# Summing seven tap products in PSUM on TensorE instead of on VectorE, for the first two blocks of a convolution with two MLPs

## The chip, the cores and the metric

One core of one Trainium2 chip. The metric is the time of one execution on the device in microseconds; the median of some runs is compared. The engines that matter here are PE (matmul; its weight loads, PEld, overlap it), VectorE (DVE in the rows), ScalarE (ACT) and the queue SP, which issues nearly all DMAs. PE reads its operands from SBUF and writes PSUM; VectorE and ScalarE read and write both.

## The reference

x is [2, 4096, 192], weight_gen is [2, 4096, 8, 7]; all is float32. Over the seven taps of each token and head a softmax is taken, and each token's output is the weighted sum of the seven tokens that end with it (zeros ahead of the sequence), 8 heads of 24 channels. Then two MLPs follow, 192 to 2048 to 192, with different activations.

```python
w = exp(weight_gen - max(weight_gen, axis=-1))
w = w / (sum(w, axis=-1) + 1e-9)
out[b, s, h, :] = sum over k of w[b, s, h, k] * x_pad[b, s + k, h, :]
x = out.reshape(8192, 192)
h = x @ moe_w_in;   x = maximum(0.01 * h, h) @ moe_w_out
h = x @ moe2_w_in;  x = maximum(h, 0) ** 2 @ moe2_w_out
```

## The kernel before

The 8192 tokens are 16 blocks of 512 (tb). A block is held as 128 partitions by 4 tokens (TB) by 192 channels for the sum over taps, and as channels by 512 tokens for the MLPs. For these every float32 operand is split into a high part (rounded to fp32r) and a low part (the rest): `xah`, `xal` hold channels 0 to 127 of a block, and `xbh`, `xbl` hold channels 128 to 191 twice, in partitions 0 to 63 and again in 64 to 127, so that two matmuls of 64 rows can run side by side as a pair. `halves` makes such a split: ScalarE casts (L359), VectorE subtracts (L366).

A block of one layer has 8 steps of 256 hidden units. A step forms `ph` (two PSUM banks) from x and the first weights (L518), ScalarE makes `gh` and `g` of it (L636 and L637 in layer one), VectorE subtracts `gl` (L644), and two steps later (LAG) PE adds the second product into `pa` and `pb` (L534). The list `steps` begins with three steps of block 0 (AHEAD = 3), then steps of blocks 1 and 0 alternate. So steps 0 to 2 belong to block 0, step 3 is the first of block 1. Steps 0 and 1 form only `ph` (nine units of matmuls); from step 2 on a step is 19 pairs.

`local_sum` makes the sum over taps of a block on VectorE: the softmax (L407 to L422), seven products, each of `xc` (the block with its halo) and one tap of `wg`, broadcast over 24 channels (L430), and an addition of each product after the first to `att` (L438). Products go through `tmp`, a ring "c" of two buffers. Then the sum has to be turned from tokens by channels to channels by tokens. Blocks 0 and 1 (`tb < EARLY`) have it turned by PE: ScalarE copies channels 128 to 191 once more behind the others (L443), and eight transposes of 128 by 128 (L451) write two tiles `pt`, for the a part and the b part. `pt` shares the PSUM ring "ph" of two slots with `ph`. The later 14 blocks are turned by VectorE's 32 by 32 transpose (L461) and a round trip through DRAM.

At the start the weights of both layers are also loaded and split (`piece`): ScalarE L283, VectorE L288 and L294, ScalarE L300, VectorE L304, then ScalarE L318 and VectorE L328 write the high and low parts. Each piece is one or two of the eight parts of a matrix.

The order of instructions on each engine is fixed when the program is built, by the class `Plan`. Every operation gives an engine, a cost in us, a priority, and the buffers that it reads and writes. PE takes its operations strictly in order of priority. The other engines take, by the planned times, the operation with the smallest priority unless another can start more than 0.15 us earlier. A buffer of a ring is given when its last user has ended in the plan. On the chip an engine works through its list in order and waits for semaphores. The products and additions have priority `pr - 2`, the transposes `at[0, tb] - 0.45` (just ahead of the block's first step), `gl` of step s has s + 1.2. For block 2 the products and additions have priority 10, ahead of the `gl` of step 9, which has 10.2. A second `xc` or `wg` is loaded when the products of the block before have been done, since each has one buffer.

Of the kernel before, what the change touches and what calls it, by code (L numbers as in the profile page):

```python
# [8 lines left out]
F32 = mybir.dt.float32  # L9
# [5 lines left out]
ALU = mybir.AluOpType  # L15
# [125 lines left out]
def kernel(  # L141
# [17 lines left out]
    nc = tc.nc  # L159
# [3 lines left out]
    B, S, D = x.shape  # L163
    H, K = weight_gen.shape[2], weight_gen.shape[3]
    G = D // H
    FF = w_in1.shape[1]
    NT = B * S
    P = 128
    HALO = K - 1
    TB = 4  # L170
    N = TB * P
    NTB = NT // N
    A = 32
# [4 lines left out]
    Q = 64  # L178
# [16 lines left out]
    def act(n):  # L195
        return 0.17 + n / 1200

    def dve(n):
        return (n + 151) / 960
# [166 lines left out]
            lambda: nc.vector.tensor_tensor(lo.t, v(), h.t.bitcast(F32), op=ALU.subtract),  # L366
        )

    AW = 4 * Q

    def local_sum(tb, pr, gate=()):
        xc = pl.buf(sb, [P, HALO + TB, D], F32, "xc", "xc", 1)
        wg = pl.buf(sb, [P, TB, H, K], F32, "wg", "wg", 1)
        mx = pl.buf(sb, [P, R, 1], F32, "mx", "mx", 1)
        sm = pl.buf(sb, [P, R, 1], F32, "sm", "sm", 1)
        att = pl.buf(sb, [P, TB, AW], F32, "att", "att", 1)
        xs = sets[0, tb] = x_set()

        xv = lambda: xc.t.rearrange("p t d -> p (t d)")

        def load_w():
            for i in range(BI):
                (nc.sync if tb else nc.scalar).dma_start(
                    out=wg.t[i * A : (i + 1) * A].rearrange("p t h k -> p (t h k)"), in_=wg_flat[i, :, tb]
                )

        def load():
            q = nc.sync
            if tb == 0:
                nc.gpsimd.memset(xc.t[0 : 2 * A, 0:HALO, :], 0.0)  # L390
            for i in range(BI):
                z = max(HALO - TB * i, 0) if tb == 0 else 0
                q.dma_start(out=xv()[i * A : (i + 1) * A, z * D :], in_=window(i, 0, A, tb, z, HALO + TB))
                for b in range(B if z else 0):
                    a0 = b * APB + 1
                    q.dma_start(  # L396
                        out=xv()[i * A + a0 : i * A + a0 + APB - 1, : z * D], in_=window(i, a0, APB - 1, 0, 0, z)
                    )

        pl.op("SP" if tb else "ACT", 2.0, pr - 10, [], [wg], load_w, after=gate, late=(0.4, 2.0))  # L400
        pl.op("SP", 2.0 if tb else 4.0, pr - 10, [], [xc], load, after=gate, late=(3.6, 2.0))

        def w2():
            return wg.t.rearrange("p t h k -> p (t h) k")

        n = R * K
        pl.op("DVE", dve(n), pr - 3, [wg], [mx], lambda: nc.vector.tensor_reduce(mx.t, w2(), axis=AX.X, op=ALU.max))  # L407
        pl.op(
            "DVE", dve(n), pr - 3, [wg, mx], [wg],
            lambda: nc.vector.tensor_tensor(w2(), w2(), mx.t.to_broadcast([P, R, K]), op=ALU.subtract),  # L410
        )
        pl.op("ACT", act(n), pr - 3, [wg], [wg], lambda: nc.scalar.activation(w2(), w2(), AF.Exp))

        def norm():
            nc.vector.tensor_reduce(sm.t, w2(), axis=AX.X, op=ALU.add)
            nc.vector.tensor_scalar_add(sm.t, sm.t, 1e-9)
            nc.vector.reciprocal(sm.t, sm.t)

        pl.op("DVE", dve(n) + 0.45, pr - 3, [wg], [sm], norm)
        pl.op(  # L420
            "DVE", dve(n), pr - 3, [wg, sm], [wg],
            lambda: nc.vector.tensor_tensor(w2(), w2(), sm.t.to_broadcast([P, R, K]), op=ALU.mult),  # L422
        )

        def acc():
            return att.t[:, :, 0:D].rearrange("p t (h g) -> p t h g", g=G)

        def prod(k, dst):
            xk = xc.t[:, k : k + TB, :].rearrange("p t (h g) -> p t h g", g=G)
            nc.vector.tensor_tensor(dst, xk, wg.t[:, :, :, k : k + 1].to_broadcast([P, TB, H, G]), op=ALU.mult)  # L430

        pl.op("DVE", dve(TB * D), pr - 2, [xc, wg], [att], lambda: prod(0, acc()))
        for k in range(1, K):
            tmp = pl.buf(sb, [P, TB, H, G], F32, "tmp", "c", 2)
            pl.op("DVE", dve(TB * D), pr - 2, [xc, wg], [tmp], lambda k=k, tmp=tmp: prod(k, tmp.t))
            pl.op(
                "DVE", dve(TB * D), pr - 2, [att, tmp], [att],
                lambda tmp=tmp: nc.vector.tensor_tensor(acc(), acc(), tmp.t, op=ALU.add),  # L438
            )

        if tb < EARLY:
            pl.op(
                "ACT", act(N // 2), pr - 1, [att], [att], lambda: nc.scalar.copy(att.t[:, :, D:AW], att.t[:, :, P:D])  # L443
            )
            for k, o in (("a", 0), ("b", P)):
                pt = pl.buf(ps, [P, 2, N], F32, "pt", "ph", 2)

                def tr(pt=pt, o=o):
                    for t in range(TB):
                        to = pt.t[:, 0, :].rearrange("p (i t a) -> p t i a", i=BI, a=A)[:, t]  # L450
                        nc.tensor.transpose(to, att.t[:, t, o : o + P], ident)  # L451

                pl.op("PE", 4 * 0.24, at[0, tb] - 0.45, [att, ident_b], [pt], tr)
                halves(xs, k, lambda pt=pt: pt.t[:, 0, :], pt, pr - 1, first=k == "a")
        else:
            J = D // 32
            xb = pl.buf(sb, [P, J, TB, 32], F32, "xb", "c", 2)
            sc = pl.buf(dram, [P, J * N // 4], F32, "sc", "sc", 2)
            pl.op(
                "DVE", dve(TB * D), pr - 2, [att], [xb],  # L460
                lambda: nc.vector.transpose(  # L461
                    xb.t.rearrange("p j t a -> p t j a"), att.t[:, :, 0:D].rearrange("p t (j b) -> p t j b", b=32)
                ),
            )
            pl.op(
                "SP", 0.5, pr - 2, [xb], [sc],
                lambda: nc.sync.dma_start(out=sc.t, in_=xb.t.rearrange("p j t a -> p (j t a)")), late=(1.5, 4.5),
            )
            for k, js in (("a", (0, 1, 2, 3)), ("b", (4, 5, 4, 5))):
                v = pl.buf(sb, [P, N], F32, "x" + k, "w", 4)  # L470

                def back(v=v, js=js):
                    for i, j in enumerate(js):
                        nc.sync.dma_start(
                            out=v.t[32 * i : 32 * i + 32].rearrange("b (i m) -> b i m", i=4),
                            in_=sc.t.rearrange("(i b) (j m) -> j b i m", b=32, j=J)[j],
                        )

                o = pl.op("SP", 2.0, pr - 2, [sc], [v, *xs.values()], back, after=taken[-1:], late=(1.0, 2.0))
                if k == "a":  # L480
                    taken.append(o)
                halves(xs, k, lambda v=v: v.t, v, pr - 1)
# [307 lines left out]
```

## Time and profile before

| | |
|---|---|
| median of 3 runs | 1163.28 us (1163.01 to 1163.58) |
| profiled execution: time, span | 1163.79 us, 1162.0 us |
| mean granted clock of PE | 0.992 |
| PE busy, instructions | 1115.8 us (96%), 9712 |
| VectorE busy | 671.5 us (58%) |
| ScalarE busy | 756.4 us (65%) |

The span is the time from the first to the last instruction of the profiled execution; 1.8 us lie around it. Shares of busy time are means over the whole span, and the start is not like the rest: PE has its first work at 21.5 us, and from 100 us on it has no gap until the last step. Matmuls overlap, so the distance between the starts of two is the better measure of their pace.

### The profile page before, as it was taken

The numbers are of one execution on the slowest core, as the hardware profiler recorded it, in microseconds if no ns is written. First come the engines' busy times: TensorE is split into PE (matmuls) and PEld (weight loads), VectorE is DVE, ScalarE is ACT, GpSimd is POOL, SyncE is SP. The second block draws the span as 40 slices with busy tenths as digits, with TensorE's granted clock in tenths as the row PEclk, the third lists the DMA queues.
The fourth block names the chain that finished last, engine by engine and source line by source line (L and its number), as shares of the span: only waits on it lengthen the run. The fifth ranks groups of instructions, "written<-read, shape, count | busy, mean of one in ns | idle before, by whom it ended". The sixth has DMA issues, their size and how long they took to land.

```text
span 1162.0 us, 23950 instructions
## 1 busy us (share of the span) xinstructions
PE 1115.8 (96%) x9712; PEld 922.0 (79%) x9712; DVE 671.5 (58%) x784; ACT 756.4 (65%) x826; POOL 1.7 (0%) x7
## 2 busy tenths in 40 slices
PE   2599999999999999999999999999999999999997
PEld 1397888888888888888888888888888888888885
DVE  7999988647374563836546383654737442333332
ACT  3574578574857657485664857657485765778775
POOL 0000000000000000000000000000000000000000
PEclk9799999999999999999999999999999999999999
DMA  7603544122203012130311203021220210010000
GB/s 185 171 2 84 139 137 116 53 51 51 67 15 102 15 42 62 28 89 15 86 26 47 62 15 102 15 67 37 55 62 15 82 33 10 25 33 15 15 16 15
DMA packets 92423, 65.52 MB, mean 56 GB/s; under 512 B 56668, under 2 KB 79226, under 8 KB 92312
## 3 DMA queue, kind: packets, MB, share of 16 engines
q1 hardware_dynamic: 92120, 63.87, 21.6%
q8 instruction: 77, 1.26, 0.4%
q14 instruction: 34, 0.28, 0.1%
q10 hardware_dynamic: 192, 0.11, 0.0%
HBM read 45.86 MB, written 18.09 MB: 55 GB/s over the span
## 4 chain that ended last, share of the span: by engine, by line
PE 94%; DVE 4%; ACT 1%; DMA 0%; issue 0%; SPq 0%; POOL 0%; DVEq 0%; ACTq 0%; POOLq 0%
PE ph L518 44%; PE pa L534 30%; PE pb L534 20%; DVE att L438 1%; DVE tmp L430 1%; DVE gl L644 0%; DMA xc<-in_x_dram 0%; DVE wa L294 0%; ACT g L637 0%; DVE att L430 0%; SPq L396 0%; DVE wa L304 0%; DVE wi0l L328 0%; DVE wa L288 0%; DVEq L785 0%
## 5 line engine op out<-in xcount | busy, mean ns | idle before, releaser
L534 PE MATMUL pa<-gh,wo 64*128 64x512 f32 x2040 | 586.0, 387 | 0.0
L644 DVE TENSOR_TENSOR gl<-g,gh 128x1024 fp32r<-128x1024 f32 x256 | 313.4, 1224 | 463.5 <-ACT g L641 362.7
L534 PEld LDWEIGHTS pa<-gh,wo 64*128 64x128 f32 x2040 | 376.3, 185 | 39.5
L534 PE MATMUL pb<-gl,wo 64*128 64x512 f32 x1020 | 313.6, 387 | 4.1 <-DVE gl L644 4.1
L534 PE MATMUL pb<-gh,wo 64*128 64x512 f32 x1020 | 313.5, 387 | 0.0
L534 PE MATMUL pa<-gl,wo 64*128 64x512 f32 x1020 | 313.5, 387 | 0.0
L636 ACT ACTIVATE gh<-ph 128x1024 fp32r<-128x1024 f32 x128 | 131.5, 1028 | 215.2 <-PE ph L518 214.9
L534 PEld LDWEIGHTS pb<-gl,wo 64*128 64x128 f32 x1020 | 188.1, 185 | 24.6 <-DVE gl L644 4.9
L639 ACT ACTIVATE g<-ph 128x1024 f32<-128x1024 f32 x128 | 131.5, 1028 | 111.6 <-PE ph L518 110.8
L534 PEld LDWEIGHTS pb<-gh,wo 64*128 64x128 f32 x1020 | 188.0, 185 | 20.0 <-issue 0.4
L534 PEld LDWEIGHTS pa<-gl,wo 64*128 64x128 f32 x1020 | 188.2, 185 | 19.8
L518 PE MATMUL ph<-xal,wi0h 64*128 64x512 f32 (+1 forms) x508 | 149.3, 389 | 0.0
L518 PE MATMUL ph<-xal,wi1h 64*128 64x512 f32 x512 | 148.7, 386 | 0.0
L640 ACT ACTIVATE gh<-g 128x1024 fp32r<-128x1024 f32 x128 | 135.7, 1060 | 4.0
L641 ACT ACTIVATE g<-g 128x1024 f32<-128x1024 f32 x128 | 135.7, 1060 | 4.0
L637 ACT ACTIVATE g<-ph 128x1024 f32<-128x1024 f32 x128 | 130.6, 1020 | 0.0
L518 PE MATMUL ph<-xah,wi0h 64*128 64x512 f32 (+1 forms) x508 | 102.0, 392 | 2.5 <-ACT wi0h L318 1.9
L518 PE MATMUL ph<-xah,wi0l 64*128 64x512 f32 (+1 forms) x508 | 101.2, 389 | 1.9 <-DVE wi0l L328 1.7
L518 PE MATMUL ph<-xah,wi1l 64*128 64x512 f32 x512 | 99.7, 386 | 0.0
L518 PE MATMUL ph<-xah,wi1h 64*128 64x512 f32 x512 | 99.7, 386 | 0.0
L518 PE MATMUL ph<-xbl,wi0h 64*128 64x512 f32 x256 | 98.8, 390 | 0.0
L518 PE MATMUL ph<-xbl,wi1h 64*128 64x512 f32 x256 | 98.8, 386 | 0.0
(68 smaller groups left out, 1245.9 us busy)
## 6 DMA issues: line engine op xcount, KB each, us to landing
xc<-in_x_dram SPq DMA_DIRECT2D x62, 240.0 KB, 4.6
raw<-in_moe_w_out_dram SPq DMA_DIRECT2D x7, 768.0 KB, 5.6
sc<-xb SPq DMA_DIRECT2D x14, 384.0 KB, 2.4
ka<-s SPq DMA_DIRECT2D x16, 256.0 KB, 2.0
sa<-ka SPq DMA_DIRECT2D x16, 256.0 KB, 3.2
su<-kb SPq DMA_DIRECT2D x32, 128.0 KB, 2.8
out_dram<-ta SPq DMA_DIRECT2D x64, 64.0 KB, 2.0
raw<-in_moe_w_in_dram SPq DMA_DIRECT2D x7, 512.0 KB, 5.3
```

What stands on the lines that cost most here:

```text
L430: nc.vector.tensor_tensor(dst, xk, wg.t[:, :, :, k : k + 1].to_broadcast([P, TB, H, G]), op=ALU.mult)
L438: lambda tmp=tmp: nc.vector.tensor_tensor(acc(), acc(), tmp.t, op=ALU.add),
L518: return nc.tensor.matmul(ph.t[:, bank, :], lhsT=wi[l][whl][r, j, sl, :], rhs=xs[xk].t[r], start=start, stop=stop)
L534: return nc.tensor.matmul((pb if k == "b" else pa).t, lhsT=wo[l2][r, 2 * j2 + c, COLS[k]], rhs=g.t[r, c, :], start=start, stop=stop,)
L636: pl.op("ACT", W, pr, [ph], [gh], lambda: nc.scalar.activation(gh.t, ph.t, AF.Prelu, alpha=0.01))
L637: pl.op("ACT", W, pr, [ph], [g], lambda: nc.scalar.activation(g.t, ph.t, AF.Prelu, alpha=0.01))
L639: pl.op("ACT", W, pr, [ph], [g], lambda: nc.scalar.activation(g.t, ph.t, AF.Relu))
L640: pl.op("ACT", W, pr, [g], [gh], lambda: nc.scalar.activation(gh.t, g.t, AF.Square))
L641: pl.op("ACT", W, pr, [g], [g], lambda: nc.scalar.activation(g.t, g.t, AF.Square))
L644: lambda: nc.vector.tensor_tensor(gl.t, g.t, gh.t.bitcast(F32), op=ALU.subtract),
```

## The change

For blocks 0 and 1 VectorE makes all seven products into `tmp`, the first too. PE turns each of them with eight transposes into one tile `pt` of two banks, one for channels 0 to 127 and one for channels 64 to 191. The first product's transposes start the accumulation in a bank (`start` at the first of the four), and those of the six others add to it. So the six additions on VectorE and ScalarE's copy of `att` are gone. The a part is split as before. Channels 128 to 191 lie in the upper half of the second bank only, so ScalarE makes `xbh` by two copies of 64 partitions, VectorE subtracts for the upper half of `xbl`, and ScalarE copies this to the lower half. The plan's cost of a turn of eight transposes is 1.2 us. Blocks 2 to 15 keep their additions; `att` has 192 columns for 256.

```diff
@@ -366,14 +366,12 @@
             lambda: nc.vector.tensor_tensor(lo.t, v(), h.t.bitcast(F32), op=ALU.subtract),
         )
 
-    AW = 4 * Q
-
     def local_sum(tb, pr, gate=()):
         xc = pl.buf(sb, [P, HALO + TB, D], F32, "xc", "xc", 1)
         wg = pl.buf(sb, [P, TB, H, K], F32, "wg", "wg", 1)
         mx = pl.buf(sb, [P, R, 1], F32, "mx", "mx", 1)
         sm = pl.buf(sb, [P, R, 1], F32, "sm", "sm", 1)
-        att = pl.buf(sb, [P, TB, AW], F32, "att", "att", 1)
+        att = pl.buf(sb, [P, TB, D], F32, "att", "att", 1)
         xs = sets[0, tb] = x_set()
 
         xv = lambda: xc.t.rearrange("p t d -> p (t d)")
@@ -423,43 +421,58 @@
         )
 
         def acc():
-            return att.t[:, :, 0:D].rearrange("p t (h g) -> p t h g", g=G)
+            return att.t.rearrange("p t (h g) -> p t h g", g=G)
 
         def prod(k, dst):
             xk = xc.t[:, k : k + TB, :].rearrange("p t (h g) -> p t h g", g=G)
             nc.vector.tensor_tensor(dst, xk, wg.t[:, :, :, k : k + 1].to_broadcast([P, TB, H, G]), op=ALU.mult)
 
-        pl.op("DVE", dve(TB * D), pr - 2, [xc, wg], [att], lambda: prod(0, acc()))
-        for k in range(1, K):
-            tmp = pl.buf(sb, [P, TB, H, G], F32, "tmp", "c", 2)
-            pl.op("DVE", dve(TB * D), pr - 2, [xc, wg], [tmp], lambda k=k, tmp=tmp: prod(k, tmp.t))
+        if tb < EARLY:
+
+            pt = pl.buf(ps, [P, 2, N], F32, "pt", "ph", 2)
+
+            def turn(k, tmp):
+                v = tmp.t.rearrange("p t h g -> p t (h g)")
+                for i in range(2):
+                    for t in range(TB):
+                        nc.tensor.matmul(
+                            pt.t[:, i, :].rearrange("p (i t a) -> p t i a", i=BI, a=A)[:, t],
+                            lhsT=v[:, t, Q * i : Q * i + P], rhs=ident, is_transpose=True,
+                            start=k == 0 and t == 0, stop=k == K - 1 and t == TB - 1,
+                        )
+
+            for k in range(K):
+                tmp = pl.buf(sb, [P, TB, H, G], F32, "tmp", "c", 2)
+                pl.op("DVE", dve(TB * D), pr - 2, [xc, wg], [tmp], lambda k=k, tmp=tmp: prod(k, tmp.t))
+                pl.op(
+                    "PE", 2 * TB * 0.15, at[0, tb] - 0.45 + 0.01 * k, [tmp, ident_b], [pt],
+                    lambda k=k, tmp=tmp: turn(k, tmp),
+                )
+            halves(xs, "a", lambda: pt.t[:, 0, :], pt, pr - 1, first=True)
+            bh, bl = xs["bh"], xs["bl"]
+            for r in HALVES:
+                pl.op("ACT", act(N), pr - 1, [pt], [bh], lambda r=r: nc.scalar.copy(bh.t[r], pt.t[Q:P, 1, :]))
             pl.op(
-                "DVE", dve(TB * D), pr - 2, [att, tmp], [att],
-                lambda tmp=tmp: nc.vector.tensor_tensor(acc(), acc(), tmp.t, op=ALU.add),
+                "DVE", dve(N), pr - 1, [pt, bh], [bl],
+                lambda: nc.vector.tensor_tensor(bl.t[Q:P], pt.t[Q:P, 1, :], bh.t[Q:P].bitcast(F32), op=ALU.subtract),
             )
-
-        if tb < EARLY:
-            pl.op(
-                "ACT", act(N // 2), pr - 1, [att], [att], lambda: nc.scalar.copy(att.t[:, :, D:AW], att.t[:, :, P:D])
-            )
-            for k, o in (("a", 0), ("b", P)):
-                pt = pl.buf(ps, [P, 2, N], F32, "pt", "ph", 2)
-
-                def tr(pt=pt, o=o):
-                    for t in range(TB):
-                        to = pt.t[:, 0, :].rearrange("p (i t a) -> p t i a", i=BI, a=A)[:, t]
-                        nc.tensor.transpose(to, att.t[:, t, o : o + P], ident)
-
-                pl.op("PE", 4 * 0.24, at[0, tb] - 0.45, [att, ident_b], [pt], tr)
-                halves(xs, k, lambda pt=pt: pt.t[:, 0, :], pt, pr - 1, first=k == "a")
+            pl.op("ACT", act(N), pr - 1, [bl], [bl], lambda: nc.scalar.copy(bl.t[0:Q], bl.t[Q:P].bitcast(F32)))
         else:
+            pl.op("DVE", dve(TB * D), pr - 2, [xc, wg], [att], lambda: prod(0, acc()))
+            for k in range(1, K):
+                tmp = pl.buf(sb, [P, TB, H, G], F32, "tmp", "c", 2)
+                pl.op("DVE", dve(TB * D), pr - 2, [xc, wg], [tmp], lambda k=k, tmp=tmp: prod(k, tmp.t))
+                pl.op(
+                    "DVE", dve(TB * D), pr - 2, [att, tmp], [att],
+                    lambda tmp=tmp: nc.vector.tensor_tensor(acc(), acc(), tmp.t, op=ALU.add),
+                )
             J = D // 32
             xb = pl.buf(sb, [P, J, TB, 32], F32, "xb", "c", 2)
             sc = pl.buf(dram, [P, J * N // 4], F32, "sc", "sc", 2)
             pl.op(
                 "DVE", dve(TB * D), pr - 2, [att], [xb],
                 lambda: nc.vector.transpose(
-                    xb.t.rearrange("p j t a -> p t j a"), att.t[:, :, 0:D].rearrange("p t (j b) -> p t j b", b=32)
+                    xb.t.rearrange("p j t a -> p t j a"), att.t.rearrange("p t (j b) -> p t j b", b=32)
                 ),
             )
             pl.op(
```

## Rows read from the trace of the kernel before

**Rows 1.** The page, first part: busy time, share of the span, instructions.
```profile
PE 1115.8 (96%) x9712; PEld 922.0 (79%) x9712; DVE 671.5 (58%) x784; ACT 756.4 (65%) x826; POOL 1.7 (0%) x7
```

**Rows 2.** Waits of PE, 0 to 120 us: total us, times, longest.
```profile
PE pt L451 <- DVE att L438: 31.4, 2, 21.6
PE pb L534 <- DVE gl L644: 2.4, 1, 2.4
PE ph L518 <- ACT wi0h L318: 1.9, 2, 1.4
PE ph L518 <- DVE wi0l L328: 1.7, 1, 1.7
```

**Rows 3.** Timeline from 0 us: start, duration, instruction, idle time before it and releaser.
```profile
9.30 0.96 DVE L430 TENSOR_TENSOR att<-xc,wg 128x768 f32<-128x768 f32 x1 [1.71 <-DMA xc<-in_x_dram]
...
21.57 1.94 PE L451 MATMUL pt<-ident,att 128*128 128x128 f32 x8 [21.57 <-DVE att L438]
...
24.94 0.80 PE L518 MATMUL ph<-xah,wi0h 128*128 128x512 f32 x1 [1.43 <-ACT wi0h L318]
...
29.88 0.56 PE L518 MATMUL ph<-xah,wi0h 128*128 128x512 f32 x1
```

**Rows 4.** Timeline of PE around block 1's transposes.
```profile
38.97 0.39 PE L534 MATMUL pa<-gh,wo 64*128 64x512 f32 x1
...
39.20 0.39 PE L534 MATMUL pa<-gh,wo 64*128 64x512 f32 x1
...
49.44 1.94 PE L451 MATMUL pt<-ident,att 128*128 128x128 f32 x8 [9.85 <-DVE att L438]
51.95 0.79 PE L518 MATMUL ph<-xah,wi0h 64*128 64x512 f32 x2 [0.57 <-DVE xal L366]
52.81 0.80 PE L518 MATMUL ph<-xbh,wi0h 64*128 64x512 f32 x2
```

**Rows 5.** Groups by line and shape, 0 to 60 us: busy us, mean ns, idle before.
```profile
L438 DVE TENSOR_TENSOR att<-att,tmp 128x768 f32<-128x768 f32 x12 | 11.5, 958 | 0.4
L430 DVE TENSOR_TENSOR tmp<-xc,wg 128x768 f32<-128x768 f32 x12 | 11.4, 952 | 0.0
```

**Rows 6.** Windows: length, busy of the five engines, PE's granted clock, DMA share, GB/s.
```profile
43.50:44.00 0.50, 0.00 (x0) 0.00 (x0) 0.50 (x2) 0.50 (x1) 0.00 (x0) 0.69 0.00 0
...
49.00:51.50 2.50, 1.94 (x8) 1.57 (x8) 2.47 (x6) 1.11 (x3) 0.00 (x0) 0.50 0.47 89
...
54.00:57.00 3.00, 3.00 (x18) 2.15 (x16) 3.00 (x5) 0.76 (x1) 0.00 (x0) 0.50 0.98 231
57.00:60.00 3.00, 3.00 (x28) 2.62 (x26) 2.93 (x5) 1.54 (x2) 0.00 (x0) 0.94 0.40 132
...
95.00:98.50 3.50, 3.50 (x20) 2.71 (x20) 2.88 (x5) 0.53 (x1) 0.00 (x0) 0.53 1.04 241
```

**Rows 7.** Chain of work, 75 to 95 us: start, us, instruction.
```profile
90.61 0.97 DVE att L438
...
92.51 1.19 DVE gl L644
```

**Rows 8.** Timeline of PE after 93 us.
```profile
93.74 0.50 PE L534 MATMUL pb<-gl,wo 64*128 64x512 f32 x1 [2.44 <-DVE gl L644]
...
95.14 0.62 PE L534 MATMUL pa<-gh,wo 64*128 64x512 f32 x1
...
95.57 0.62 PE L534 MATMUL pa<-gh,wo 64*128 64x512 f32 x1
...
98.13 0.47 PE L518 MATMUL ph<-xbh,wi0h 64*128 64x512 f32 x2
```

**Rows 9.** Instructions of three lines: ns min/median/max, first and last start us.
```profile
L451 PE MATMUL pt<-ident,att x16: 421/421/446, 21.6 to 51.0; 128*128 128x128 f32 x16
L359 ACT CAST xah<-pt x2: 586/586/586, 23.0 to 50.6; 128x512 fp32r<-128x512 f32 x2
...
L653 ACT COPY u<-pb x32: 583/583/586, 110.7 to 1154.4; 64x512 f32<-64x512 f32 x32
```

## The prediction

> **What bounds the kernel now.** I read the page first: PE is busy 96% of the span [rows 1]. So the rest of the kernel runs at PE's pace, and an edit to the start is worth what it takes off PE's idle time there, and no more. I then asked who made PE wait in the first 120 us [rows 2]: 31.4 us in two waits on VectorE's last addition of `att` (one per block that PE transposes; the first, 21.6 us, is the whole start), 3.6 us on weights being split, and 2.4 us on one `gl`. After 120 us PE stands idle only in the tail, which the change doesn't touch. So the sum is made in the stretch up to about 100 us, and what is gained there moves the end by the same amount.
>
> Next the timeline. Block 0: the first product starts at 9.30, the eight transposes wait for the last addition and take 1.94 us from 21.57, and step 0 starts at 24.94, having waited for the ACT cast of its weight [rows 3]. Block 1: PE is through step 2 at 39.59, stands for 9.85 us, transposes at 49.44, starts step 3 at 51.95, and its second pair (which needs `xbh`) at 52.81 [rows 4]. VectorE is the reason: twelve products and twelve additions of 0.95 us each [rows 5] stand in one line with the weight splitting.
>
> Third, PE's clock. In 43.50 to 44.00 the granted clock is 0.69 on its way from 1.00 to 0.50 (1.2 GHz), so it fell about 4 us after PE stopped at 39.59. It is 0.50 through the second burst of transposes and in 54 to 57, and 0.94 in 57 to 60 [rows 6]. The first burst takes the same 1.94 us [rows 3], so it ran at the low level too, although the clock row has no entry for it.
>
> Last, a later wait that belongs to the same engine: VectorE does block 2's additions ahead of a `gl`, PE waits 2.44 us for it, and after that wait the clock is 0.53 in 95.0 to 98.5 [rows 6 to 8], where pairs follow each other by 0.43 us [rows 8] instead of 0.23 [rows 4].
>
> **The change part by part.** *Removed from VectorE:* twelve additions of 0.957 us, 11.5 us; with a product each addition makes up a period of about 1.86 us. Everything that VectorE does in both kernels (seven products per block, both subtractions of a block, all weight work) costs what it did.
>
> *Added to PE:* seven turns of eight transposes for one burst of eight, 48 more per block. From the burst, (1.94 - 0.42) / 7 = 0.217 us each at the low clock (0.42 is the last one's own length [rows 9]), so 1.74 us for a turn. No row shows a transpose at the high clock. Below it is bounded by half of 0.217 (0.108, if it halves with the clock), above by 0.217 (if the load of the stationary operand sets it). A pair of 512 columns goes from 0.43 to 0.23 [rows 4, 8], so I take 0.13 us, about 1.0 us for a turn.
>
> *New wait:* two `tmp` buffers are shared, so product k+2 waits until turn k has read its buffer. While the turn takes 1.74 us and the product 0.95 us, PE paces the line, and VectorE has 0.8 us free in each period. Queued behind the waiting product is weight work. The plan costs a turn at 1.2 us, so it puts small weight pieces (0.35 to 0.56 us) into part of these gaps, and the rest is idle: I estimate 2 us in block 0 and 1 us in block 1.
>
> *Where the turns lie.* Block 0: product 0 is done at 10.25; turns then follow each other until 10.4 + 7 x 1.74 = 22.6. The cast `xah` (0.59 us) starts at about 22.8, so step 0 starts at 23.5 instead of 24.94. The weights no longer hold it, since the splitting that stood behind the additions now runs in the gaps. Gain so far 1.4 us: on a cold PE seven turns take as long as the thirteen VectorE instructions that they shorten.
>
> Steps 0 to 2: nine units of 0.43 us are 3.9 us at the low clock; step 1 takes 3.5 us with the clock rising on the way (it rose 4 to 5 us after step 0 began before); step 2 takes 4.3 us plus the change of row group. Before, the stretch took 39.59 - 24.94 = 14.6 us, because step 2 waited for its weights [rows 2]; VectorE is now some 3 to 5 us earlier with them, so I count 12.0 us and let step 2 end at 35.5.
>
> Block 1: the turns are in PE's fixed order behind step 2, so the first starts at 35.5. Two products lie ready. PE has been at full clock, and I assume it keeps it for the 4 us that it kept it when idle: two turns by 37.6, then about 1.2 us for each (a product of 0.95 us must follow each turn, with waits and some weight work between) until 40.0, which makes four turns; the last three at 1.74 us end at 45.2. Then `xah` and two half-row copies for `xbh`. A 64-row copy of 512 columns takes the time of a cast of 128 rows, 0.58 us [rows 9], so that is 0.6 + 1.1 us after pt is done at 45.4: the second pair of step 3 starts at 47.2 instead of 52.81. **Gain 5.6 us.**
>
> *Moved or added beside it:* ACT loses the copy of `att` and gains one half copy for `xbh` and the copy of `bl`, under 2 x 0.58 us a block; the part on the path is already in the 1.1 us above. The copy of `bl` back to rows 0 to 63 has the first four pairs of the step as cover; without that it would cost 0.6 us a block. The DMAs of x and the weights are the same; block 1's load waits for the last product, which moves by under 1 us, and block 1's turns wait for PE anyway. pt holds one slot of the PSUM ring of two through the turns; step 2 has the other, and step 3 comes after the turns, so nothing waits for it. A narrower `att` costs nothing: no instruction reads its copied columns.
>
> *The `gl` wait at 91.* VectorE has 11.5 us less to do and PE arrives only 5.6 us earlier; with some 3 us of idle time in the gaps, VectorE is about 2.9 us further ahead of PE (1.5 to 4). The wait of 2.44 us then goes, and with it the low clock behind it: from 95.14 to 98.13 seven pairs took 2.99 us that take 1.59 at 0.227, and with the edges 1.6 us. An idle stretch of 1.73 us at 33.7 to 35.4 [rows 2] did not lower the clock (the pairs at 39 us follow by 0.23 [rows 4]), so a remnant under a microsecond wouldn't either. I take 2.1 of the 2.44 us and the 1.6 us: 3.7 us.
>
> Sum: 5.6 + 3.7 = 9.3 us off 1163.8 (the profiled execution; its span is 1162.0, and the median shown is 1163.28) gives 1154.5.
>
> **The clock in a stretch of transposes** decides between 4 us more or less. Rows: from the first matmul after the transposes the low clock lasted from 24.94 to about 29.6 and from 51.95 to about 57.0, 4.7 and 5.1 us; after the `gl` wait, with no transposes ahead, from 93.74 to 98.13, 4.4 us [rows 3, 4, 6, 8]. A burst ahead did not bring the rise forward. That speaks for transposes that don't raise the clock, but two bursts of under 2 us are weak evidence. The Trainium skill ("TensorE: Matmul & The Clock Gate", Part 4: PE-mode transpose) says the full clock doesn't engage for transposes, since they don't count as PE activity in the same way. By that rule the sum stays at 1154.5; without it, the second rival's time holds. No run here shows a long stretch of them yet.
>
> **The rivals.**
> *The `gl` wait stays.* VectorE's order is written by the plan, and the plan puts all of block 2's sum before that `gl`. If its slack grows by under a microsecond, the wait and the low clock stay: 1163.8 - 5.6 = 1158.2. For it: the order is fixed by costs that know no clock. Against it: 11.5 us less work.
>
> *Transposes hold the clock up.* Then block 0 has three turns at 1.74 us and four at about 1.3, step 0 starts near 21.7 at full speed, step 2 ends near 32, block 1 stays at 1.2 us a turn, and the second pair of step 3 comes near 42.5. That is 10.3 us, and 2 us more since step 3 no longer runs at 0.43 us a pair for 5 us; VectorE's lead over PE is gone, so the `gl` wait stays: about 1151.5.
>
> *No high-clock turns at all.* If transposes never take less than 0.217 us, or the clock falls before block 1's turns, these take 12.2 us: step 3 at about 49.5, gain 3.3, and the lead of VectorE is larger, 3.3 to 4 us of the `gl` wait with its clock: 1156.5 to 1160.5.
>
> *Slower: a transpose that adds costs more than one that writes.* The two chains together are 2 x 56 transposes, so with no turn at the high clock step 3's second pair starts at 11.3 + 112 s + 14.0 us for a cost of s each (11.3 is 10.4 and the 0.9 to step 0; 14.0 is the 12.0 of steps 0 to 2 and the 2.0 from the last turn to that pair). It equals 52.81 at s = 0.246, only 13% over the row's 0.217. At 0.30 it would be 58.9, 6 us later: 1170. Against it: an accumulating matmul of ph follows the first one at the same 0.43 us at the low clock, and its transposes load the same operands.
>
> **How the numbers follow.** Chances: the forecast 0.36; the `gl` wait stays 0.24; the clock held up 0.22; only slow turns 0.09; slower 0.06; no change, because something that I don't see (a weight that lands late) holds step 3, 0.03. The range takes in the first three and most of the fourth, with the bounds of a turn at the high clock (0.9 to 1.74 us, about 1 us in the sum either way): 1150.5 to 1160.0, with about 0.85 inside. Below 0.2% (2.3 us, about what a measurement of this kernel tells from no change) lie the first four: faster 0.91, same 0.03, slower 0.06.
>
> **What the profile after would show.** Right: no `att` additions before block 2; turns of 1.7 us from 10.4 to 22.6; step 0 near 23.5; PE's wait before step 3 replaced by turns that start near 35.5; step 3 near 46 to 47 at 0.50; no wait for `gl` near 86, and a clock of 1.00 after it. Wrong: transposes at 0.11 us before 20 us (second rival), a `gl` wait of over 1.5 us (first), or spacings over 0.25 us (last). The forecast fails most easily at the plan's order, since one product more ahead of the `gl` is worth 0.95 us and the clock behind it 1.6.

## The result, and the profile after

The changed kernel takes 1153.35 us (median of 4 runs, 1153.05 to 1153.56) where the kernel before takes 1163.14; the ratio is 0.9916, interval 0.9904 to 0.9928. That is 9.8 us less, and in the profiled executions 1163.79 to 1153.05, 10.7 us, of which 9.3 were forecast. First the page after: the span, and busy time by engine.

```profile
span 1151.3 us, 24139 instructions
...
PE 1123.9 (98%) x9808; PEld 926.4 (80%) x9808; DVE 660.3 (57%) x772; ACT 758.6 (66%) x828; POOL 1.7 (0%) x7
```

VectorE has 11.2 us less to do than in [rows 1], 96 matmul instructions more stand on PE, and the span is shorter by 10.7 us. Where it went is read from the second pair of a step (`xbh` with the high weight), at which [rows 4] also stops. Before, in the timeline of PE, for steps 4, 11 and 13:

```profile
59.38 0.42 PE L518 MATMUL ph<-xbh,wi0h 64*128 64x512 f32 x2
...
89.53 0.42 PE L518 MATMUL ph<-xbh,wi0h 64*128 64x512 f32 x2
...
102.56 0.39 PE L518 MATMUL ph<-xbh,wi0h 64*128 64x512 f32 x2
```

And after, in the same view, the turns of block 0, steps 0 and 2, the turns of block 1, then steps 3, 4, 11 and 13:

```profile
10.31 6.88 PE L438 MATMUL pt<-ident,tmp 128*128 128x128 f32 x40 [10.31 <-DVE tmp L428]
17.43 1.97 PE L438 MATMUL pt<-ident,tmp 128*128 128x128 f32 x16 [0.24 <-DVE tmp L428]
20.88 0.50 PE L531 MATMUL ph<-xah,wi0h 128*128 128x512 f32 x1 [1.48 <-ACT xah L359]
...
30.42 0.50 PE L531 MATMUL ph<-xah,wi0h 64*128 64x512 f32 x2 [2.97 <-ACT wi0h L318]
...
37.85 1.97 PE L438 MATMUL pt<-ident,tmp 128*128 128x128 f32 x16
...
44.49 1.09 PE L438 MATMUL pt<-ident,tmp 128*128 128x128 f32 x8 [0.18 <-DVE tmp L428]
46.26 0.50 PE L531 MATMUL ph<-xah,wi0h 64*128 64x512 f32 x2 [0.67 <-ACT xah L359]
46.87 1.10 PE L531 MATMUL ph<-xbh,wi0h 64*128 64x512 f32 x2
...
53.11 0.39 PE L531 MATMUL ph<-xbh,wi0h 64*128 64x512 f32 x2
...
83.25 0.39 PE L531 MATMUL ph<-xbh,wi0h 64*128 64x512 f32 x2
...
91.87 0.39 PE L531 MATMUL ph<-xbh,wi0h 64*128 64x512 f32 x2
```

Step 3 comes 5.94 us earlier (52.81 to 46.87), step 4 6.27, step 11 still 6.28, and step 13 10.69. So the gain was made in two places, 6.3 us by step 4 and 4.4 us at the `gl` of step 9 (2.4 of them the wait for it, the rest the low clock behind it); after that nothing changes any more up to the end.

VectorE at that second place, before, is first shown at the `gl` of step 8, which waits for ScalarE's `g` (timeline):

```profile
82.90 1.22 DVE L644 TENSOR_TENSOR gl<-g,gh 128x1024 fp32r<-128x1024 f32 x1 [0.35 <-ACT g L637]
```

And after, from the `gl` of step 8 to that of step 9, with block 2's 32 by 32 transpose between them:

```profile
76.76 1.22 DVE L657 TENSOR_TENSOR gl<-g,gh 128x1024 fp32r<-128x1024 f32 x1
77.90 0.95 DVE L467 TENSOR_TENSOR att<-att,tmp 128x768 f32<-128x768 f32 x1
78.77 0.95 DVE L428 TENSOR_TENSOR tmp<-xc,wg 128x768 f32<-128x768 f32 x1
79.75 0.96 DVE L467 TENSOR_TENSOR att<-att,tmp 128x768 f32<-128x768 f32 x1
80.74 0.98 DVE L474 STREAM_TRANSPOSE xb<-att 128x768 f32<-128x768 f32 x1
81.64 1.18 DVE L657 TENSOR_TENSOR gl<-g,gh 128x1024 fp32r<-128x1024 f32 x1
```

As in [rows 7], the end of block 2's sum stands ahead of the `gl` of step 9. But the order isn't the same: four instructions of block 2 stand between the two `gl` now, where there were nine (four products, four additions, the transpose). The plan, in whose times VectorE has less work, puts block 2's first product behind the `gl` of step 5 (65.31 us), where it came behind that of step 6 (76.78 us). So this `gl` starts 1.4 us ahead of step 11 (83.03), where it started 3.2 us behind it (92.51 against 89.30), which is 4.6 us in VectorE's favour. PE waits for nothing there, and the low clock of [rows 6, 8] is gone (1.00 from 82 to 94 us). What PE waits for after, 0 to 120 us:

```profile
PE pt L438 <- DVE tmp L428: 11.3, 5, 10.3
PE ph L531 <- ACT wi0h L318: 3.0, 1, 3.0
PE ph L531 <- ACT xah L359: 2.2, 2, 1.5
PE ph L531 <- ACT xbl L459: 1.2, 2, 0.9
...
PE pb L547 <- DVE gl L657: 0.5, 1, 0.5
```

Of the 31.4 us in [rows 2] the first product's 10.3 us are left, and 1.0 us between turns. Longer is the wait ahead of step 2, for a weight that ScalarE casts: 2.97 us, where it was 0.48. New are 1.2 us in two waits for the copy of `bl` (L459), one in each block. The clock in and after the wait for the weight, and in block 1's turns and step 3 (windows; granted clock third from the right):

```profile
30.00:31.00 1.00, 0.58 (x4) 0.30 (x4) 1.00 (x3) 1.00 (x3) 0.00 (x0) 1.00 1.14 234
...
32.00:33.00 1.00, 1.00 (x6) 0.81 (x8) 1.00 (x4) 1.00 (x2) 0.00 (x0) 0.50 1.07 375
...
35.00:36.00 1.00, 0.86 (x8) 0.73 (x10) 1.00 (x4) 0.43 (x1) 0.00 (x0) 1.00 0.34 74
...
37.80:42.00 4.20, 3.98 (x34) 3.45 (x32) 4.20 (x6) 4.20 (x6) 0.00 (x0) 1.00 0.57 185
42.00:46.00 4.00, 3.06 (x24) 2.58 (x24) 4.00 (x6) 1.61 (x3) 0.00 (x0) 1.00 0.05 13
...
46.00:48.00 2.00, 1.53 (x7) 0.85 (x8) 1.55 (x3) 1.92 (x4) 0.00 (x0) 1.00 0.56 121
48.00:50.00 2.00, 1.13 (x9) 0.57 (x8) 1.94 (x4) 1.07 (x3) 0.00 (x0) 1.00 1.04 246
```

The wait before step 2 cost the clock too: step 2 runs at 1.2 GHz from 31.3 to 34.7. The 8 us of transposes after it did not, and step 3 has the full clock. One line's instructions (ns, min/median/max) say what a transpose takes:

```profile
L438 PE MATMUL pt<-ident,tmp x112: 272/273/472, 10.3 to 45.3; 128*128 128x128 f32 x112
```

Sixteen take 1.97 us, so (1.97 - 0.27) / 15 = 0.113 us from start to start at the high clock, and a turn at least 0.9 us. Of the first forty, 18 took 4.08 us, 24 took 4.75 us, and the last 16 2.1 us. Nothing but transposes had run on PE until then, and their pace doubled.

### The profile page after: what moved, and what is told of

It reads as the page before. It is cut to its first block, busy times and chain, and to the rows that moved or that the text cites. A ratio compares the mean times of both kernels' runs of the same rounds, so it can differ in the third digit from the quotient of the medians.

```text
span 1151.3 us, 24139 instructions
## 1 busy us (share of the span) xinstructions
PE 1123.9 (98%) x9808; PEld 926.4 (80%) x9808; DVE 660.3 (57%) x772; ACT 758.6 (66%) x828; POOL 1.7 (0%) x7
## 4 chain that ended last, share of the span: by engine, by line
PE 95%; DVE 2%; ACT 1%; issue 0%; DMA 0%; SPq 0%; POOL 0%; DVEq 0%; POOLq 0%; ACTq 0%
PE ph L531 45%; PE pa L547 30%; PE pb L547 20%; DVE tmp L428 1%; PE pt L438 1%; DMA xc<-in_x_dram 0%; DVE gl L657 0%; DVE wa L294 0%; DVE wa L304 0%; ACT xbh L454 0%; DVE wo L328 0%; SPq L394 0%; ACT wu L300 0%; DVE xbl L457 0%; DVE xal L366 0%
```

## The experiments

Twelve kernels, each against the kernel before on the same chip. Five came out above both times that had been expected for them (the `gl` first, the cast first, three buffers, the softmax later, the cheaper turn), one below (the warm start). "Step 3", "step 4" and "step 13" are again the second pairs of these steps.

**Block 0 alone.** The turns for block 0, additions and one burst for block 1 (`att` 256 columns wide again, with its copy).

```diff
-        if tb < EARLY:
+        if tb == 0:
...
+            if tb < EARLY:
...
+                    pl.op("PE", 4 * 0.24, at[0, tb] - 0.45, [att, ident_b], [pt], tr)
```

> Only block 0 has its products turned and added by PE; block 1 keeps its six additions. If the gain at the start is VectorE's line of work: step 0 starts near 21 as in the changed kernel, step 2 still waits for its weights, block 1's sum is done 4 us earlier than before, step 3 starts near 48 at the low clock (PE stands for 7 us ahead of it), and the gl wait stays at 1 to 2.5 us: 1157.5 to 1159.5 us. If instead the gain is the clock that the turns hold up through block 1: under 2 us are left of it here, 1161.5 to 1163.

Measured 1161.05 us, ratio 0.9981 (0.9971 to 0.9990): 2 us. That lies between the two expected ranges, 0.5 us from the second, by which the clock would be the gain. The rows that show what stood in the way, in PE's waits (the profiled execution, 1162.06 us, is among the slowest of ten, 1159.08 to 1162.15):

```profile
PE pb L562 <- DVE gl L672: 11.4, 1, 11.4
```

and in the timeline of VectorE:

```profile
43.81 0.96 DVE L467 TENSOR_TENSOR att<-att,tmp 128x768 f32<-128x768 f32 x1
44.68 1.22 DVE L672 TENSOR_TENSOR gl<-g,gh 128x1024 fp32r<-128x1024 f32 x1
```

Step 2 starts at 30.94 and then stands for 11.4 us: with its weights done earlier, the plan puts all of block 1's sum ahead of the `gl` of step 0. Step 3 comes at 55.19, later than before. The 2 us that are left come from the second place: PE does not wait for the `gl` of step 9.

**Block 0 alone, with that `gl` first.** Block 1's sum at a priority 0.3 larger.

```diff
+        if tb == 1:
+            pr += 0.3
```

> As the run with block 0 alone, with block 1's sum at a priority 0.3 larger, so that VectorE makes the gl of step 0 ahead of the thirteen instructions of block 1's sum. If the 11.4 us that PE waited there are a matter of this order: the wait goes, step 2 ends near 36, and block 1's sum, which ends at about the same time as there plus one gl, sets step 3 near 54 all the same: 1160 to 1162, since VectorE's line still bounds it. If block 0's saving can reach the end without block 1's: 1157 to 1159.

Measured 1161.53 us, 0.9986 (0.9977 to 0.9995). That is in the first of the expected ranges. The 11.4 us are gone, and PE waits 8.0 us for block 1's last addition instead, and 2.8 us for a cast of ScalarE ahead of step 3. That step comes at 51.38, 1.4 us earlier than before, and the wait for the `gl` of step 9 is back in full, 2.5 us. So block 0's turns alone are worth almost nothing: block 1's sum behind them stands in the same line on VectorE.

**Block 1 alone.** The same edit with `tb == 1`.

> Only block 1 has its products turned and added by PE. If VectorE's line of work is it: steps 0 to 2 are as before and end near 39.6, the seven turns follow at 1.1 us each, step 3 starts near 48 at the high clock, so step 4 comes 4 to 5 us earlier; VectorE's lead grows by about 1 us, so that the gl wait shrinks and may go with the low clock behind it: 1155 to 1159 us. If transposes did not hold the clock, the last turns would take 1.7 us each and step 3 run at 0.43 us a pair: 1159 to 1161.

Measured 1157.96 us, 0.9954 (0.9939 to 0.9969), as expected in time. The PE timeline shows a longer way to it: block 1's last turns and the start of step 3.

```profile
45.19 1.97 PE L438 MATMUL pt<-ident,tmp 128*128 128x128 f32 x16 [0.69 <-DVE tmp L428]
48.06 1.09 PE L438 MATMUL pt<-ident,tmp 128*128 128x128 f32 x8 [0.91 <-DVE tmp L428]
49.83 0.50 PE L546 MATMUL ph<-xah,wi0h 64*128 64x512 f32 x2 [0.67 <-ACT xah L359]
50.44 0.49 PE L546 MATMUL ph<-xbh,wi0h 64*128 64x512 f32 x1
51.78 0.50 PE L546 MATMUL ph<-xbh,wi0h 64*128 64x512 f32 x1 [0.85 <-ACT xbh L454]
```

The turns start at 40.38 and end at 49, since VectorE still has weight work and a `gl` between the products. After waits of 0.7 to 0.9 us one after the other the clock fell in step 3, to 0.50 from 53 to 55 us, so step 4 comes only 1.5 us earlier. The other 4.4 us are the `gl` wait, which is gone. The two halves (1.9 and 5.0 us) add up to less than the whole (9.8).

**The kernel before, with block 2's sum behind the `gl` of step 9.**

```diff
+        if tb == EARLY:
+            pr += 0.5
```

> The kernel before, with block 2's sum at a priority behind the gl of step 9 (0.5 more), nothing else. If the second term of the prediction is a matter of VectorE's order alone, the wait of 2.44 us and the low clock behind it (2.0 us) go without the change: 1158.5 to 1159.5 us. If block 2's x is needed as early as it was made, another wait takes its place: 1162 to 1164.

Measured 1168.36 us, 1.0042 (1.0027 to 1.0057): slower, and above both expectations. The wait for that `gl` is gone, and step 13 comes 4.1 us earlier (98.49 for 102.56). PE waits 0.4 us for the next `gl`, and then twice at block 2's first steps, in the timeline of PE:

```profile
113.91 0.50 PE L520 MATMUL ph<-xbh,wi0h 64*128 64x512 f32 x2 [2.34 <-ACT xbh L359]
...
118.00 0.79 PE L520 MATMUL ph<-xbl,wi0h 64*128 64x512 f32 x1 [2.65 <-DVE xbl L366]
```

The loads of `xb` are issued at 109.24 us, where the kernel before issues them at 97.24. Block 2's sum has to be early, and so has the `gl`: this order gave the 4 us, and lost more behind them. An order that puts more of block 2's sum ahead of the `gl` of step 8, as the changed kernel has it, was not tried without the change.

**The same, with PE kept at transposes.** 64 transposes of the identity go ahead of block 1's own; their output is overwritten.

```diff
+                    for _ in range(64 if tb and not o else 0):
+                        nc.tensor.transpose(pt.t[:, 0, 0:P], ident, ident)
```

> As the run with the gl first, and PE makes 64 further transposes of the identity into pt ahead of block 1's own, in the 9.85 us in which it stood idle; their output is overwritten. If transposes hold the clock: it stays at 1.00 from 39.6 through step 3, which then takes 5 us instead of 7.2, so 2 us off the run with the gl first: 1156.3 to 1157.5 us. If transposes do not count: the clock falls near 43.7 all the same and the time is that of the run with the gl first, within 0.5 us, or more by what the slower transposes then take.

Measured 1167.52 us, 1.0039 (1.0025 to 1.0053); the two intervals overlap, so the time decides nothing. The windows do. With the transposes:

```profile
43.00:44.00 1.00, 1.00 (x12) 1.00 (x10) 1.00 (x2) 1.00 (x2) 0.00 (x0) 1.00 0.00 0
...
47.00:48.00 1.00, 0.93 (x9) 0.69 (x7) 0.97 (x3) 0.00 (x0) 0.00 (x0) 1.00 0.00 0
...
53.00:54.00 1.00, 1.00 (x6) 0.42 (x4) 1.00 (x2) 0.48 (x1) 0.00 (x0) 0.50 1.06 238
```

without them:

```profile
43.00:44.00 1.00, 0.00 (x0) 0.00 (x0) 1.00 (x2) 1.00 (x2) 0.00 (x0) 0.50 0.00 0
```

Transposes hold the clock where an idle PE loses it. They ended at 47.9, and after waits of 1.0, 1.5 and 0.4 us the clock fell at 52.7, in the first pairs of the step that was to have it.

**Warm start.** The changed kernel, with 36 transposes of the identity while PE waits for the first product.

```diff
+                for _ in range(36 if tb == 0 and k == 0 else 0):
+                    nc.tensor.transpose(pt.t[:, 0, 0:P], ident, ident)
```

> The changed kernel, in which PE makes 36 transposes of the identity in its idle time before the first product (their output is overwritten). If transposes raise the clock: block 0's turns start at 0.123 us a transpose instead of 0.217 and end near 18 us instead of 19.4, step 0 starts 1 to 1.5 us earlier; if step 2 is bound by its weights, nothing of it is left behind step 2: 1152.5 to 1153.8 us. If transposes did not count, block 0's turns start at 1.7 us each as in the changed kernel.

Measured 1151.63 us (1151.44 to 1151.87), 0.9901 (0.9888 to 0.9915): 1.7 us below the changed kernel and 0.9 us below the low end of what was expected. It is the fastest of all; its runs lie below all of the changed kernel's, though the two ratios (each against the kernel before on its own chip) overlap in their intervals. In PE's timeline:

```profile
1.36 6.12 PE L437 MATMUL pt<-ident 128*128 128x128 f32 x36 [1.36 <-POOL ident masks.py:199]
10.19 1.97 PE L440 MATMUL pt<-ident,tmp 128*128 128x128 f32 x16 [2.71 <-DVE tmp L428]
```

The first product's turns run at the high clock, which only transposes can have raised. Step 0 starts at 19.45 instead of 20.88, step 2 at 28.98 instead of 30.42, and this 1.43 us stays to the end (span 1149.9). So the wait for the weight moved along: VectorE's work behind the products starts earlier when these wait less for turns (0.32 us, 1.67 in the changed kernel). That PE could gain nothing ahead of step 2 was wrong.

**The cast for step 2 first.** The changed kernel; ScalarE's cast of that weight 0.6 higher in priority.

```diff
-        pl.op("ACT", act(n), pr - 1, [wa], [hb], high, after=tuple(borrowed) if l else ())
+        pl.op("ACT", act(n), pr - (1.6 if (kind, l, j) == ("i", 0, 2) else 1), [wa], [hb], high, after=tuple(borrowed) if l else ())
```

> The changed kernel, with ScalarE's cast of the weight that step 2 begins with (the piece of parts 2 and 3 of the first matrix) 0.6 higher in priority, so that it comes ahead of g of step 0 and the softmax of block 1. If the early steps are now bound by the order of the weight splitting: PE's wait of 2.97 us ahead of step 2 shrinks by 1.5 to 2 us, the clock does not fall in it, step 2 ends 2 to 4 us earlier and so does all that follows, unless the gl wait comes back: 1149.5 to 1151.5 us. If VectorE as a whole is the bound there: 1152.5 to 1154.

Ratio 0.9924 (0.9907 to 0.9940; 1154.72 us where before took 1163.96): no gain, above both expectations. Step 2 starts at 30.40, now held by `g` of step 0, which had to make room (1.3 us, since its `ph` is still being read), and then waits 3.1 us for the `gl` made of it. ScalarE has little idle time there (0.39 us from 26.5 to 30.4 in the changed kernel), and the order chooses what waits. But the trace differs ahead of the edit too: block 0's first forty transposes take 7.53 us (6.88 in the changed kernel), step 0 starts 0.9 us later, and the clock is 0.50 from 23 to 26 us, so not all of the loss is shown to be the order's.

**The same, with block 2's sum behind the `gl`.** Both edits above.

> The same with block 2's sum behind the gl of step 9 as well. If that gl wait came back in the run with the cast first: this one is faster than it by the wait and the low clock behind it. If it did not come back: the two are the same within 0.4 us.

Ratio 0.9964 (0.9954 to 0.9975), slower than with the cast alone: the wait for the `gl` of step 9 had not come back there, and the wait for `xbh` at block 2's first step (2.34 us at 112.58) came as it did when the kernel before had this order. The profiled execution (1162.54 us) is the slowest of seven, whose median is 1158.93; its clock is also 0.50 from 31 to 41 us, in step 2 and block 1's first turns, which the others need not share.

**Three product buffers** instead of two.

```diff
-                tmp = pl.buf(sb, [P, TB, H, G], F32, "tmp", "c", 2)
+                tmp = pl.buf(sb, [P, TB, H, G], F32, "tmp", "c", 3)
```

The ring "c" also serves the products of the later blocks, `xb` and `ta`; these lines have 3 for 2 as well and are left out here.

> The changed kernel with three buffers for the products instead of two. If the waits for a buffer cost what the trace shows (0.2, 0.37 and 0.18 us between block 1's turns; in block 0 the turns follow each other anyway): up to 0.8 us less, 1152.4 to 1153.3 us. If the product is what a turn waits for: no change, 1153.1 to 1153.6.

Ratio 0.9926 (0.9911 to 0.9941; 1154.91 us): not faster, and above both expectations. The waits between turns went, and step 3 came at 45.72 instead of 46.87. But ScalarE was busy with other work when the turns ended; PE stood for 2.0 us ahead of step 3, and its clock fell at 48.1. Step 4 came at 53.38, 0.3 us later than without, and at the `gl` of step 9 PE waited 0.6 us, so that step 13 came 1.2 us later.

**Block 1's softmax later.** Its five operations at priority 1.1 instead of 0.

```diff
+        sp = 1.9 if tb == 1 else 3
...
-        pl.op("DVE", dve(n), pr - 3, [wg], [mx], lambda: nc.vector.tensor_reduce(mx.t, w2(), axis=AX.X, op=ALU.max))
+        pl.op("DVE", dve(n), pr - sp, [wg], [mx], lambda: nc.vector.tensor_reduce(mx.t, w2(), axis=AX.X, op=ALU.max))
```

> The changed kernel with block 1's softmax at priority 1.1 instead of 0, so that the weights of step 2 and the gl of step 0 come ahead of it. If the early steps wait for the order of the weight work: step 2 starts about 1 us earlier than at 30.42, does not fall to the low clock, and ends 1 to 3 us earlier; block 1's two first products come later but still before step 2's end, so all after it is 1 to 2 us earlier: 1151 to 1152.5 us. If block 1's products now set the first turn: no gain, 1153 to 1155.

Median 1156.18 us, 0.9931 (0.9918 to 0.9944), with five runs from 1152.39 to 1156.73, far wider than the changed kernel's. The profiled one (1156.27) has step 3 at 46.78, as early as the changed kernel, and the low clock in it (windows):

```profile
48.00:50.00 2.00, 1.26 (x7) 0.67 (x7) 1.90 (x4) 1.59 (x3) 0.00 (x0) 0.77 1.01 234
50.00:52.00 2.00, 1.99 (x10) 1.60 (x12) 1.97 (x3) 0.69 (x1) 0.00 (x0) 0.50 0.68 139
```

Step 4 comes at 56.28, 3.2 us later than in the changed kernel. The mean granted clock of the five runs goes with their time: 0.998 at 1152.39 us, 0.996 at 1153.91, 0.994 at 1156.18 to 1156.73. So the same instructions keep the clock in one execution and lose it in another.

**The plan's cost of a turn at 0.96 us** instead of 1.2.

```diff
-                    "PE", 2 * TB * 0.15, at[0, tb] - 0.45 + 0.01 * k, [tmp, ident_b], [pt],
+                    "PE", 2 * TB * 0.12, at[0, tb] - 0.45 + 0.01 * k, [tmp, ident_b], [pt],
```

> The changed kernel with the plan's cost of a turn at 0.96 us, near what it takes at the high clock (0.98), instead of 1.2. VectorE then has its products one behind the other, without weight work between them, and the gl of step 0 ahead of block 1's first products. If that order is what holds step 2 and the turns: 0.5 to 2 us less, 1151.3 to 1152.8. If the weight work that is pushed back holds step 0 and step 2 instead: 1153.5 to 1156.

Median 1156.78 us, 0.9944 (0.9931 to 0.9956). The products follow each other as expected, the weight work behind them holds step 0 until 22.80 (3.5 us), step 3 comes at 46.02 and runs at the low clock, and a wait of 1.2 us for the `gl` of step 9 returns.

**Warm start, with the `gl` of step 0 first and the gap ahead of step 2 filled.** The attempt at a version better still.

```diff
+            for _ in range(18):
+                nc.tensor.transpose(junk.t[:, 0:P], ident, ident)
+        pl.op("PE", 0.05, 1.5, [ident_b], [junk], fn)
...
-                pl.op("DVE", dve(TB * D), pr - 2, [xc, wg], [tmp], lambda k=k, tmp=tmp: prod(k, tmp.t))
+                pl.op("DVE", dve(TB * D), pr - (1.7 if tb else 2), [xc, wg], [tmp], lambda k=k, tmp=tmp: prod(k, tmp.t))
```

> As the warm start, with 18 further transposes of the identity ahead of step 2 (into a PSUM buffer that nobody reads, in the 3 us in which PE stands there), and block 1's products at priority 1.3 instead of 1, so that VectorE makes the gl of step 0 ahead of the first two of them. If step 2 is held by that gl and by the low clock after the gap: the clock stays up, step 2 ends 1.5 us earlier than at 36.4 and all after it as well: 1149.8 to 1150.8 us. If the new order pushes other weight work behind the turns: a wait in step 4 or later takes it back, 1151.5 to 1154.

Measured 1153.80 us, 0.9919 (0.9905 to 0.9933): 2.2 us above the warm start by the medians, though the intervals of the ratios overlap. The clock stays at 1.00 through step 2, and its `gl` is no wait any more. But the warm start gave nothing in the profiled run: the 36 transposes took 5.54 us (6.12 in the warm start alone), PE stood for 3.50 us behind them (2.71), the clock is 0.77 in 10 to 12 us and 0.50 in 12 to 14, and block 0's first 32 transposes take 5.38 us. The last turns wait 0.7 and 0.9 us for products behind weight work, and the clock falls in step 3 (0.58 in 48 to 52).

## Why the prediction was right, and where its terms were not

The forecast of 1154.5 lies 1.2 us from the median and names both places where the time came from; it counts from the profiled execution (1163.8), and as a difference it is 9.3 us against 9.8. But its first term, 5.6 us against 5.94 at step 3, came out of errors that cancel, so that its size is luck:

- *Turns of block 0.* Forecast 12.2 us for seven at the low clock, to 22.6; measured 10.31 to 19.40, 9.1 us. The forecast let the low clock last; the pace doubled after 18 transposes, some 4 us. Step 0 came at 20.88 instead of 23.5, 2.6 us early.
- *Steps 0 to 2.* Forecast 12.0 us, measured 17.0 (20.88 to 37.9). This is the step that failed most. Steps 0 and 1 took 6.6 us (7.4 forecast), then PE stood for 2.97 us, and step 2 took 7.5 us (4.6 forecast). "VectorE is now some 3 to 5 us earlier with them" left ScalarE out: the first pair of step 2 came 2.6 us earlier than before (30.42 for 32.98), the one that needs VectorE's low part 3.7 us (31.73 for 35.44). ScalarE's timeline after:

```profile
26.50 1.03 ACT L649 ACTIVATE gh<-ph 128x1024 fp32r<-128x1024 f32 x1
27.42 1.02 ACT L650 ACTIVATE g<-ph 128x1024 f32<-128x1024 f32 x1
28.32 0.39 ACT L410 ACTIVATE wg<-wg 128x224 f32<-128x224 f32 x1
29.10 0.54 ACT L300 ACTIVATE wu<-raw 128x384 int32<-128x384 uint32 x1 [0.39 <-DVE wa L294]
29.55 0.81 ACT L318 CAST wi0h<-wa 128x768 fp32r<-128x768 f32 x1
```

  VectorE had made `wa` for this cast at 26.9, and the cast came at 29.55. The run with the cast first speaks against the order alone: there `g` comes late and `gl` with it. In step 2 itself PE waits 0.58 us for `wi0l` and 0.48 us for a `gl`, and the clock is low until 34.7. Step 2 ended 2.4 us later than forecast, at 37.9.
- *Turns of block 1.* Forecast 9.7 us (four at about 1.2, three at 1.74), measured 7.7 (37.85 to 45.58), all at the high clock, and 1.3 us instead of 2.0 from there to the second pair. The pace of 1.1 us for a turn was the one forecast with the clock up (1.2), and it lasted.

In sum: 2.6 early, 5.0 late, 2.0 and 0.7 early, together 0.3 us early. Step 3 then ran at the full clock and not at 0.50 as forecast, yet that gave only 0.3 us more by step 4. PE waits in it for block 1's own split, 0.87 us of it for the copy of `bl`, which the forecast counted as covered by the step's first pairs.

*The clock.* The forecast took transposes as work that does not raise the clock, from two bursts under 2 us, and called that weak. It was wrong, and the second rival was right in its mechanism: the pace doubles within 36 transposes with nothing else on PE (warm start), and 64 of them hold the clock at 1.00 where it falls to 0.50 without (the kept-busy run). The Trainium skill's rule (TensorE: Matmul & The Clock Gate, Part 4: PE-mode transpose) that the full clock doesn't engage for transposes does not hold for these float32 transposes; the measurement decides. The rival's time, 1151.5, was not reached: it let step 2 end near 32 (37.9 measured), and it gave nothing for the `gl` wait, which went and gave 4.4 us.

*The `gl` wait.* Forecast 3.7 us, measured 4.4 (step 11 to step 13, 6.28 to 10.69). The size is near, but the way to it was another. The forecast let VectorE get 2.9 us further ahead of PE. In the kernel before, though, VectorE itself stands 0.35 us for `g` of step 8, so a lead gained earlier ends there; what follows is up to the plan's order. VectorE's instructions of block 2 between the `gl` of step 8 and that of step 9 are nine in the kernel before and with block 0's `gl` put first, and PE waits 2.44 and 2.47 us; seven with three product buffers and with the cheaper turn, 0.58 and 1.16 us; three to six in the changed kernel and all other runs, and PE doesn't wait at step 11. With block 0's `gl` put first six additions are gone and the wait is there in full; in the kernel before with block 2's sum behind the `gl` (three between, all additions made) it is gone; and the cheaper turn has the changed kernel's instructions in another order, and a wait again. So it was the shorter stretch written by the plan that took the wait away, and less work on VectorE acted by way of the plan. The first rival was right that the plan's order decides, and wrong that it stays. That a plan with less work would shorten this stretch was not worked out beforehand, so this term's size is in part luck too.

*The other rivals.* Only slow turns: none after 15 us. A dearer accumulation: block 1's transposes take 0.113 us where most of them add to what is there, and the 64 of the kept-busy run, which only write, (7.21 - 0.27) / 63 = 0.110 in the timeline. So adding costs next to nothing. VectorE's products waited 1.7 us for turns in block 0 (1.19 and 0.48 in its timeline), near the estimate of 2; in block 1, where 1 us was estimated, not at all.

*The two blocks need each other.* Alone they give 1.9 and 5.0 us. Block 0's saving ends at block 1's sum on VectorE, and block 1's turns wait longer for products (1.8 us in all, 0.75 in the changed kernel) if block 0's additions stay on VectorE.

Left open: why the clock outlives the waits of 0.7 to 0.9 us ahead of step 3 in the traces of the changed kernel, the warm start and the cast first and not in seven of the others (block 1 alone, the cast first with the `gl` first, three product buffers, the softmax later, the cheaper turn, the kept-busy run, the last run). Several of their waits are alike; how they lie in time was not tried by itself, and the softmax's five runs show that it isn't a matter of the kernel alone. Nor was the sum of warm start and some other order of ScalarE's early work.

## What to carry to other kernels

Before a saving on one engine is counted on the path, name the next engine in each wait that it shortens: here PE stood 3.0 us for a cast of ScalarE, with the low clock behind it, and steps 0 to 2 took 5 us more than forecast, while a second wait 40 us later gave 4.4 back. Where a plan writes the order and one engine waits for another, read the new order: count the instructions that stand ahead of the one that is waited for, since work taken out elsewhere can move them. Idle time of PE ahead of its first real work can be filled with throwaway transposes; here that was worth 1.7 us by the medians and 1.4 in the traces, for two lines. In the last run, with 3.5 us of idle time behind them, the clock had fallen again by 12 us.

## What the runs showed of the hardware

Float32 transposes of 128 by 128 raise the clock by themselves and hold it: some 0.22 us each at first (the changed kernel's first 18 in 4.08 us), 0.11 at the high level, with accumulation or without. From step 3 to step 4 the changed kernel takes 6.2 us at the full clock, and five of its variants in whose traces the clock fell in step 3 take 7.7 to 9.5 us (the cast first with the `gl` first, softmax later, three buffers, the cheaper turn, the last run). What decides it isn't shown: the last four of these began step 3 0.1 to 1.2 us earlier than the changed kernel and had step 4 0.3 to 3.2 us later, two of them with a longer wait ahead of step 3 (2.0 and 1.2 us) and two with the same (0.7 us). And one kernel kept the clock in one execution and lost it in others (softmax later, 0.998 at 1152.39 us, 0.994 at 1156.18). The time at which the clock rises differs from trace to trace as well: block 0's first forty transposes take 6.88 us in the changed kernel and 7.53 in two others (block 0 alone, the cast first), so a difference under 1 us between two traces need not be the edit's.
